# Attention scores as products of 64 rows, two heads at a time, with q and k turned before they are split

## The chip, the cores and the metric

One core of one Trainium2 chip. The metric is the device time of one execution in microseconds, the median of several runs. TensorE is PE, VectorE is DVE, ScalarE is ACT, GpSimd is POOL, and SyncE (SP) issues most of the transfers.

## The reference

Three layers follow one another: windowed attention, a mixture of eight experts with one expert per token, and a dense layer with a cosine. The change touches the attention alone.

```python
batch, n_heads, seq, head_dim = (4, 8, 576, 64)      # all float32

def _attn_ref(q, k, v):
    scores = scale * np.matmul(q, k.transpose(0, 1, 3, 2))
    rel = pos[:, None] - pos[None, :]
    bias = slopes[:, None, None] * (-np.abs(rel))[None, :, :]
    mask = (rel >= 0) & (rel < 128)
    scores = np.where(mask, scores + bias[None], -1000000000.0)
    attn = np.exp(scores - np.max(scores, axis=-1, keepdims=True))
    attn = attn / (np.sum(attn, axis=-1, keepdims=True) + 1e-09)
    return np.matmul(attn, v)

x = attn_out.transpose(0, 2, 1, 3).reshape(B * S, H * D)
x = _moe_ref(x, ...)      # logits, argmax, relu(x @ w1[e]) @ w2[e], weighted
return _moe2_ref(x, ...)  # h = x @ w_in;  (h * cos(h)) @ w_out
```

## The kernel before

**Units.** The attention is cut into 36 units (`units`): two pairs of batches (`bp`), nine row tiles of 128 tokens (`s`), two groups of four heads (`hg`). Tile `s == 4` joins the last 64 rows of both batches of a pair. Because of the window of 128, most units see two key tiles, the first and last tile of a batch one, the joined tile three (`nv` in `score`). Four units, one pair of tiles, end with the logits of 256 tokens. The expert stage can start only when the attention is done, since the tokens are sorted by expert first.

**Two-part numbers.** A float32 is held as the sum of two float32r numbers, high and low, so that a product on TensorE keeps nearly all its bits. `split` (L629) makes the two parts of q and k with two POOL instructions on rows of tokens, 128x512 each, into `qk`, where a head's 64 high and 64 low parts lie side by side. `tr` (L637) then turns each head on PE, one turn of 128 by 128 per head: 4 for q (L646), 4 for k (L653). The result has high parts in partitions 0 to 63 and low parts in 64 to 127. For q a second copy with high and low exchanged is needed: ACT copies the turned bank (L647), DVE copies one half exchanged (L649), ACT the other (L650); k takes one ACT copy (L654).

**Scores.** `score(n, hp)` (L656) does two of a unit's four heads. One head takes two products of 128 rows (L669): high with high and low with low in the first, the crossed ones in the second. For two key tiles the two heads share a bank: DVE merges the far key tile's columns into the near one's (L679), so that each token has 128 values. Then DVE adds the bias, takes the minimum and writes `sx` (L690, for each head), and ACT takes the exponential (L697).

**Turning and the product with v.** `flip(n, hp)` (L701) turns the exponentials of two heads on PE (L710, or L726 for one or three key tiles), ACT copies them to `pa` (L711, or L728), and POOL cuts them into the two triangles that belong to the two key tiles (L712, L714, 128x256 each). `pv(n, hp)` (L732) makes the products with v (L740); after the second half of a unit DVE divides by the sum (L750, one for each unit) and SP stores x. Then x is turned (L769, every second unit), split, and multiplied with the gate weights (L782).

**What sets the order.** The loop at L834 goes through 72 half units: `score` of step i, `flip` of step i - 3, `pv` of step i - 5 (LF, LP), with loads, splits and turns four units ahead (`ahead`). The instructions are issued in the order a scheduler gives them on each engine, so that on PE the half units' pieces come interleaved. Pieces of later work (x's turns, logits, ranks) wait in the list `after`, one or two for each half step. When the 32nd unit is done, `early` (L252) joins that list: it chooses the first expert and issues the fetch of its rows (`gather`, POOL) and weights. Tiles wait for their buffers: the banks S, T and P have two buffers, O and L one.

Of the kernel before, what the change touches and what calls it, by code (L numbers as in the profile page):

```python
# [15 lines left out]
ALU = mybir.AluOpType  # L16
# [13 lines left out]
def kernel(  # L30
# [53 lines left out]
    ps = ctx.enter_context(tc.tile_pool(name="ps", bufs=1, space=PSUM))  # L84

    def bank(tag, shape, dt=F32, name="bk"):
        return ps.tile(shape, dt, name=name, tag=tag, bufs=2 if tag in "TSP" else 1)
# [379 lines left out]

    with ExitStack() as c:
# [9 lines left out]
        identr = ca.tile([128, 128], F32R, name="identr")  # L478
        MARK = {"id": nc.vector.tensor_copy(identr, ident)}
# [134 lines left out]
        R, SPL, KT, QT, X, ST, PT, O = {}, {}, {}, {}, {}, {}, {}, {}  # L614
# [14 lines left out]
        def split(n):  # L629
            r = R.pop(n)  # L630
            sp_ = SPL[n] = sp.tile([128, 8, 2, D], F32R, name="qk")
            eng = nc.vector if n < 1 else nc.gpsimd
            eng.tensor_scalar(sp_[:, :, 0], r, 1.0, 0.0, op0=ALU.mult, op1=ALU.add)
            MARK["pool" if n else "dve"] = eng.tensor_tensor(sp_[:, :, 1], r, sp_[:, :, 0].bitcast(F32),
                                                             op=ALU.subtract)

        def tr(n):  # L637
            bp, s, hg = units[n]
            if s == 0:
                KT[bp, hg] = ktp.tile([128, 4, 9 * 128], F32R, name="kT")  # L640
            sp_ = SPL.pop(n)
            qT = sp.tile([128, 4, 2, 128], F32R, name="qT", bufs=6)
            QT[n] = qT
# [12 lines left out]
        def score(n, hp):  # L656
# [6 lines left out]
            nm = sm.tile([128, 2], F32, name="nm")  # L663
            sx = []

            def products(sc, j):
                h = 2 * hp + j
                for a in range(2):
                    nc.tensor.matmul(sc, QT[n][:, h, a], KT[bp, hg][:, h, 128 * t0:128 * t0 + w],  # L669
                                     start=a == 0, stop=a == 1)  # L670

            if nv == 2:


                both = bank("S", [128, 2, 256])
                for j in range(2):
                    products(both[:, j], j)
                own, other = (slice(128, 256), slice(0, 128)) if s < 4 else (slice(0, 128), slice(128, 256))
                nc.vector.copy_predicated(both[:, :, other], near.unsqueeze(1).to_broadcast([128, 2, 128]),  # L679
                                          both[:, :, own])  # L680
                w0, wv, bc = other.start, 128, 0
            for j in range(2):
                h = 2 * hp + j
                if nv == 2:
                    sc = both[:, j]
                else:
                    sc = bank("S", [128, 512])
                    products(sc[:, :w], j)
                x = sm.tile([128, 384], F32, name="sx")
                MARK["dve"] = nc.vector.tensor_tensor_reduce(  # L690
                    out=x[:, :wv], in0=sc[:, w0:w0 + wv], in1=bt[:, 4 * hg + h, bc:bc + wv], op0=ALU.add, op1=ALU.min,
                    scale=-0.125, scalar=3.0e38, accum_out=nm[:, j:j + 1])
                sx.append(x)
            p = []
            for j in range(2):
                e = sm.tile([128, 384], F32, name="e")
                MARK["act"] = nc.scalar.activation(e[:, :wv], sx[j][:, :wv], AF.Exp, bias=nm[:, j:j + 1], scale=-1.0)  # L697
                p.append(e)
            ST[n, hp] = (p, nv, t0 + f0)

        def flip(n, hp):  # L701
            p, nv, t0 = ST.pop((n, hp))
            heads = []
            if nv == 2:
                s = units[n][1]
                pp = bank("P", [128, 4, 128])
                pa = sm.tile([128, 2, 128], F32, name="pa", bufs=3)
                pT = sm.tile([128, 4, 128], F32, name="pT")
                for j in range(2):
                    nc.tensor.transpose(pp[:, j], p[j][:, 0:128], ident)  # L710
                nc.scalar.copy(pa, pp[:, 0:2])  # L711
                nc.gpsimd.affine_select(out=pT[:, 0:2], in_=pa, pattern=[[0, 2], [1, 128]], compare_op=ALU.is_ge,  # L712
                                        fill=0.0, base=0, channel_multiplier=-1)
                nc.gpsimd.affine_select(out=pT[:, 2:4], in_=pa, pattern=[[0, 2], [-1, 128]], compare_op=ALU.is_gt,  # L714
                                        fill=0.0, base=0, channel_multiplier=1)
                for j in range(2):
                    m = (pT[:, 2 + j], pT[:, j]) if s < 4 else (pT[:, j], pT[:, 2 + j])
                    heads.append((2 * hp + j, m))
                PT[n, hp] = (heads, nv, t0)
                return  # L720
            for grp in ([0, 1],) if nv < 3 else ([0], [1]):
                pp = bank("P", [128, 4, 128])
                pT = sm.tile([128, 4, 128], F32, name="pT")
                for gi, j in enumerate(grp):
                    for b in range(nv):
                        nc.tensor.transpose(pp[:, gi * nv + b], p[j][:, 128 * b:128 * b + 128], ident)  # L726
                m = len(grp) * nv
                nc.scalar.copy(pT[:, :m], pp[:, :m])  # L728
                heads += [(2 * hp + j, [pT[:, gi * nv + b] for b in range(nv)]) for gi, j in enumerate(grp)]
            PT[n, hp] = (heads, nv, t0)  # L730

        def pv(n, hp):  # L732
            bp, s, hg = units[n]
            heads, nv, t0 = PT.pop((n, hp))
            if hp == 0:
                O[n] = bank("O", [128, 4, 128])
# [5 lines left out]
            if hp == 0:  # L742
                return
# [651 lines left out]
```

## Time and profile before

| what | us |
|---|---|
| median of 3 runs (lowest, highest) | 860.01 (859.51, 861.32) |
| the profiled execution's own time | 857.24 |
| its span, first to last instruction | 855.5 |
| first unit's division starts | 25.3 |
| last unit's division starts | 196.0 |
| first turn of the expert stage starts | 200.5 |

The profiled execution took 1.7 us more than its span, and lies 2.8 us below the median of the three runs. A row of the lines view counts instructions of one kind: their busy time together, and the mean time of one. On PE the instructions overlap, because the ends are modelled and one matmul starts before the one before it has ended; what one costs PE is read from the distance between starts in the timeline, not from its mean time.

### The profile page before, as it was taken

What the parts mean: (1) busy time and instruction counts of PE and PEld (TensorE: products, weight loads), DVE (VectorE), ACT (ScalarE), POOL (GpSimd) and SP (SyncE); (2) the same over time, 40 slices, a digit from 0 to 9 for tenths busy, and PEclk for the clock granted to TensorE, in tenths of its full rate; (3) what the DMA queues carried; (4) which work ended last, traced back from release to release, by engine and by line L of the source; (5) the groups of instructions that cost most, each with busy time, mean ns of one, the idle gap of its engine ahead of it and who ended that gap; (6) DMA issues with size and microseconds to landing.
All of it is one profiled execution on the core that took longest, in us unless ns stands there. A gap on an engine that the chain in (4) does not pass through costs nothing. (4 is left out here: it accounts for less than half of the span.)

```text
span 855.5 us, 14987 instructions
## 1 busy us (share of the span) xinstructions
PE 809.7 (95%) x5269; PEld 721.3 (84%) x5269; DVE 633.4 (74%) x1496; ACT 528.1 (62%) x984; POOL 211.6 (25%) x275
## 2 busy tenths in 40 slices
PE   6899999997899999999899999999999999999996
PEld 6789988986889999999878778787788888888995
DVE  4867788776889999998657999897665555555562
ACT  6988888854356667675456576664544554445562
POOL 6765566420103223222000121111313001200100
PEclk9999999997999999999999999999999999999999
DMA  7354443108578878869733232410402001100000
GB/s 158 92 138 110 120 111 88 33 26 270 170 245 277 277 259 289 267 219 304 239 141 97 83 118 70 158 50 32 129 30 82 1 1 35 40 1 1 25 26 25
DMA packets 125136, 103.42 MB, mean 121 GB/s; under 512 B 61725, under 2 KB 105027, under 8 KB 125059
## 3 DMA queue, kind: packets, MB, share of 16 engines
q1 hardware_dynamic: 122099, 92.74, 35.7%
q0 software_dynamic: 2960, 9.70, 3.2%
q8 instruction: 42, 0.69, 0.3%
q14 instruction: 35, 0.29, 0.1%
HBM read 85.90 MB, written 16.52 MB: 120 GB/s over the span
## 5 line engine op out<-in xcount | busy, mean ns | idle before, releaser
L1009 PE MATMUL bk<-hh,s 128*128 128x256 f32 x864 | 117.8, 284 | 8.1 <-DVE y L1009 4.1
L1009 POOL TENSOR_TENSOR lf<-lf,mag 128x512 f32<-128x512 f32 x32 | 47.7, 1491 | 282.6 <-DVE mag L1009 261.0
L1009 PE MATMUL bk<-xT,s 128*128 128x256 f32 x864 | 115.0, 282 | 2.6 <-DVE s L1009 1.9
L1009 PEld LDWEIGHTS bk<-hh,s 128*128 128x128 f32 x864 | 108.0, 188 | 10.4 <-DVE y L1009 5.1
L1009 PEld LDWEIGHTS bk<-xT,s 128*128 128x128 f32 x864 | 107.3, 188 | 3.6 <-DVE s L1009 2.3
L1009 ACT CAST s<-r 128x1024 fp32r<-128x1024 f32 x72 | 75.1, 1050 | 56.1 <-DMA r<-in_moe_w_dram 37.0
L1009 PE MATMUL bk<-yT,wi_a 128*128 128x512 f32 (+1 forms) x480 | 104.3, 368 | 1.2 <-DVE yT L1009 0.8
L1009 DVE TENSOR_TENSOR s<-r,s 128x1024 fp32r<-128x1024 f32 x72 | 95.2, 1323 | 13.8 <-ACT s L1009 13.1
L1009 PE MATMUL bk<-yT,wi_b 128*128 128x512 f32 (+1 forms) x480 | 105.0, 368 | 0.0
L1009 ACT ACTIVATE r<-r 128x512 f32<-128x512 f32 (+1 forms) x80 | 47.2, 589 | 93.7 <-DVE r L1009 93.7
L1009 PEld LDWEIGHTS bk<-yT,wi_a 128*128 128x128 f32 x480 | 84.0, 188 | 17.1 <-DVE yT L1009 1.1
L1009 PEld LDWEIGHTS bk<-yT,wi_b 128*128 128x128 f32 x480 | 84.7, 188 | 15.6
L1009 DVE TENSOR_TENSOR r<-bk,r 128x512 f32<-128x512 f32 (+1 forms) x80 | 50.9, 636 | 61.5 <-ACT r L1009 61.0
L1009 PE MATMUL bk<-wo_b,gg 128*128 128x512 f32 x384 | 93.7, 392 | 1.6 <-DVE po L1009 1.0
L1009 PE MATMUL bk<-wo_a,gg 128*128 128x512 f32 x384 | 92.4, 389 | 0.3 <-DVE gg L1009 0.3
L1009 PEld LDWEIGHTS bk<-wo_b,gg 128*128 128x128 f32 x384 | 71.4, 188 | 18.9 <-issue 1.3
L1009 PEld LDWEIGHTS bk<-wo_a,gg 128*128 128x128 f32 x384 | 72.0, 188 | 15.7 <-DVE gg L1009 0.7
L740 PE MATMUL bk<-vt,pT 128*128 128x65 f32 x544 | 71.5, 274 | 1.9 <-POOL pT L714 0.8
L1009 DVE TENSOR_TENSOR gg<-r,gg 128x512 fp32r<-128x512 f32 x64 | 46.0, 719 | 34.3 <-ACT gg L1009 34.3
L740 PEld LDWEIGHTS bk<-vt,pT 128*128 128x128 f32 x544 | 67.6, 194 | 3.2 <-issue 1.5
L669 PE MATMUL bk<-kT,qT 128*128 128x256 f32 (+2 forms) x288 | 61.9, 326 | 3.3 <-DVE nm L690 2.1
L1009 ACT CAST gg<-r 128x512 fp32r<-128x512 f32 x64 | 39.7, 620 | 41.0 <-DVE r L1009 39.8
(286 smaller groups left out, 1413.9 us busy)
## 6 DMA issues: line engine op xcount, KB each, us to landing
r<-in_moe_w_dram SPq DMA_DIRECT2D x72, 512.0 KB
y_dram<-y SPq DMA_DIRECT2D x19, 256.0 KB
rqk<-in_q_dram SPq DMA_DIRECT2D x32, 128.0 KB
rqk<-in_k_dram SPq DMA_DIRECT2D x32, 128.0 KB
vt<-in_v_dram SPq DMA_DIRECT2D x32, 128.0 KB
x_dram<-xt SPq DMA_DIRECT2D x16, 256.0 KB
f64x<-in_moe_w_in_dram SPq DMA_DIRECT2D x8, 512.0 KB
raw<-in_moe_w_dram SPq DMA_DIRECT2D x8, 512.0 KB
```

The source lines that it names most:

```text
L669: nc.tensor.matmul(sc, QT[n][:, h, a], KT[bp, hg][:, h, 128 * t0:128 * t0 + w], start=a == 0, stop=a == 1)
L740: nc.tensor.matmul(ot[:, h, 0:65], pT[b], vt_of(bp, t0 + b, hg)[:, 65 * h:65 * h + 65], start=b == 0, stop=b == nv - 1)
L1009: r = op(*args, **kwargs)
```

## The change

`tr` now turns the raw q and k: one turn of 128 by 128 float32 numbers holds two heads of 64, so 4 turns do the q and k of a unit's four heads. The turned bank is split afterwards. For the first two units ACT and DVE do that from the bank. For the others ACT copies the high part of q (128x256) and the whole bank (`rT`, 128x512), and POOL makes the high and low of k and the low of q from `rT`, three instructions of 128x256. `split`, the exchanged copies and `identr` are gone.

The two heads of a pair lie in partitions 0 to 63 and 64 to 127. `score` does a whole unit: for each pair of heads three products (high-high, high-low, low-high) of 64 rows, the two heads one after the other in the two halves, each into a bank of its own. That is 12 products of 64 rows where 8 of 128 rows were. DVE's work on the scores is the same in number and size; the merge takes the two heads of one half together. `flip` and `pv` do a whole unit too: one copy of 128x512 and two POOL cuts of 128x512 for the units with two key tiles.

The loop goes through units: `score(n)`, turns of unit n + 4, `flip(n - 1)`, `pv(n - 2)`, and `issue_after` holds the order of PE: the products of `score` stand behind all PE work of the step before, and the rest of the step stands behind them (for n < 33). From n = 33 on, a step takes up to four pieces of the list `after`. The banks S have three buffers, P one, until the attention is done.

```diff
+    banks(S=3, T=2, P=1, O=1)
...
         def tr(n):
...
-            pt = bank("T", [128, 4, 128], F32R)
-            for h in range(4):
-                nc.tensor.transpose(pt[:, h], sp_[:, h].rearrange("p a d -> p (a d)"), identr)
-            nc.scalar.copy(qT[:, :, 0], pt)
-
-            nc.vector.tensor_copy(qT[0:64, :, 1], pt[64:128])
-            nc.scalar.copy(qT[64:128, :, 1], pt[0:64])
-            pt = bank("T", [128, 4, 128], F32R)
-            for h in range(4):
-                nc.tensor.transpose(pt[:, h], sp_[:, 4 + h].rearrange("p a d -> p (a d)"), identr)
-            nc.scalar.copy(KT[bp, hg][:, :, 128 * s:128 * s + 128], pt)
...
+            pt = bank("T", [128, 4, 128])
+            for c in range(4):
+                nc.tensor.transpose(pt[:, c], r[:, 2 * c:2 * c + 2].rearrange("p a d -> p (a d)"), ident)
...
+            rT = sp.tile([128, 4, 128], F32, name="rT")
+            nc.scalar.copy(qT[:, 0], pt[:, 0:2])
+            nc.scalar.copy(rT, pt)
+            nc.gpsimd.tensor_scalar(kT[:, 0], rT[:, 2:4], 1.0, 0.0, op0=ALU.mult, op1=ALU.add)
+            nc.gpsimd.tensor_tensor(kT[:, 1], rT[:, 2:4], kT[:, 0].bitcast(F32), op=ALU.subtract)
+            MARK["pool"] = nc.gpsimd.tensor_tensor(qT[:, 1], rT[:, 0:2], qT[:, 0].bitcast(F32), op=ALU.subtract)
...
-                for a in range(2):
-                    nc.tensor.matmul(sc, QT[n][:, h, a], KT[bp, hg][:, h, 128 * t0:128 * t0 + w],
-                                     start=a == 0, stop=a == 1)
...
+                for p in pairs:
+                    for a, b in ((0, 0), (0, 1), (1, 0)):
+                        for j in range(2):
+                            rs = slice(64 * j, 64 * j + 64)
+                            with ExitStack() as w_:
+                                for ins in TURN if n < 33 else ():
+                                    w_.enter_context(tc.issue_after(ins.ins))
+                                TURN.clear()
+                                nc.tensor.matmul(sc[j][:, p - pairs[0], :w], qT[rs, a, p], kT[rs, b, p],
+                                                 start=a == 0 and b == 0, stop=a == 1)
...
+            for pairs in ([0, 1],) if nv < 3 else ([0], [1]):
+                sc = [bank("S", [128, 2, 256] if nv < 3 else [128, 1, 512]) for j in range(2)]
+                products(sc, pairs)
...
+                nc.scalar.copy(pT, pp)
...
+                nc.gpsimd.affine_select(out=tri_[0], in_=pa, pattern=[[0, 4], [1, 128]], compare_op=ALU.is_ge,
                                         fill=0.0, base=0, channel_multiplier=-1)
...
-        LF, LP = 3, 5
...
+        LF, LP = 1, 2
...
+        for n in range(N + LP):
+            if n < 3:
+                ahead(n, dt=n + 1)
+            if n < N:
+                score(n)
+            with ExitStack() as w:
+                if n < 33:
+                    w.enter_context(tc.issue_after(TURN[-1].ins))
+                setups(2 * n)
+                if n > 1:
+                    ahead(n + 1)
+                pops(1 if n < 33 else 2)
+                if LF <= n < N + LF:
+                    flip(n - LF)
+                setups(2 * n + 1)
+                if n >= LP:
+                    pv(n - LP)
+                pops(2 if 33 <= n < N + LP - 1 else 1)
+
+    nc = tc.nc
+    banks(S=2, T=2, P=2, O=1)
```

**The order on PE**, in the middle of the attention where tiles with one key tile are done. `kT,qT` are scores, `identr,qk` or `ident,rqk` the turns of q and k, `ident,e` the turns of the exponentials, `vt,pT` the products with v, `ident,xt` the turns of x. Before:

```order
L669 MATMUL bk<-kT,qT 128x256 x4
L710 MATMUL bk<-ident,e 128x128 x2
L653 MATMUL bk<-identr,qk 128x128 x4
L646 MATMUL bk<-identr,qk 128x128 x4
L653 MATMUL bk<-identr,qk 128x128 x4
L669 MATMUL bk<-kT,qT 128x256 x4
L710 MATMUL bk<-ident,e 128x128 x2
L740 MATMUL bk<-vt_139,pT 128x65 x4
L769 MATMUL bk<-ident,xt 128x128
```

Now (the line is that of the recording helper for all of them):

```order
L487 MATMUL bk<-kT,qT 128x256 x12
L487 MATMUL bk<-ident,rqk 128x128 x4
L487 MATMUL bk<-ident,e_1867 128x128 x4
L487 MATMUL bk<-vt_139,pT 128x65 x4
L487 MATMUL bk<-kT,qT 128x256 x12
L487 MATMUL bk<-ident,rqk 128x128 x4
L487 MATMUL bk<-ident,e_1956 128x128 x4
L487 MATMUL bk<-vt_140,pT 128x65 x4
L487 MATMUL bk<-ident,xt 128x128 x4
L487 MATMUL bk<-kT,qT 128x256 x12
```

The scores of a unit stand in one block, and each block stands between turns that use all 128 rows; all other work of the step follows in one fixed order.

**The order on ACT**, two steps of units with two key tiles. `e` are exponentials, `pa` copies of their turned form, `qT`, `kT`, `rT` copies of turned q and k, `xT` of turned x. Before:

```order
L697 ACTIVATE e<-sx,nm 128x128 x2
L650 COPY qT<-bk 64x4x128
L711 COPY pa<-bk 128x256
L697 ACTIVATE e<-sx,nm 128x128 x2
L647 COPY qT<-bk 128x4x128
L711 COPY pa<-bk 128x256 x2
L697 ACTIVATE e<-sx,nm 128x128 x2
L770 CAST xT_95<-bk 128x4x128
L650 COPY qT<-bk 64x4x128
L697 ACTIVATE e<-sx,nm 128x128
L654 COPY kT<-bk 128x4x128
```

Now:

```order
L679 CAST qT<-bk 128x256
L680 COPY rT<-bk 128x512
L727 ACTIVATE e_1365<-sx,nm 128x128 x4
L741 COPY pa<-bk 128x512
L789 CAST xT_98<-bk 128x4x128
L679 CAST qT<-bk 128x256
L680 COPY rT<-bk 128x512
L727 ACTIVATE e_1444<-sx,nm 128x128 x4
```

The one copy `pa` of a unit stands behind the four exponentials of the unit after it: the copy behind `e_1365` is that of the unit before `e_1365`, whose turns PE has behind the scores of `e_1365`.

## Rows read from the trace of the kernel before

**Rows 1.** Page, part 1: busy time of each engine over the span.
```profile
PE 809.7 (95%) x5269; PEld 721.3 (84%) x5269; DVE 633.4 (74%) x1496; ACT 528.1 (62%) x984; POOL 211.6 (25%) x275
```

**Rows 2.** Windows: width, busy us (instructions) PE, PEld, DVE, ACT, POOL, PEclk, DMA.
```profile
40.00:160.00 120.00, 115.06 (x1024) 107.31 (x1023) 91.65 (x428) 101.05 (x246) 71.16 (x115) 1.00 0.42 105
...
195.00:205.00 10.00, 5.78 (x27) 3.88 (x26) 5.06 (x8) 4.69 (x7) 0.85 (x1) 0.59 1.03 354
```

**Rows 3.** Timeline, DVE: the first and last unit's division (36 in all).
```profile
25.30 0.41 DVE L750 TENSOR_TENSOR xt<-bk,den 128x256 f32<-128x256 f32 x1
...
195.99 0.42 DVE L750 TENSOR_TENSOR y<-bk,den 128x256 f32<-128x256 f32 x1
```

**Rows 4.** Lines, each shape apart, 40 to 160 us: busy us, mean ns of one.
```profile
L697 ACT ACTIVATE e<-sx,nm 128x128 f32<-128x128 f32 x79 | 29.6, 404 | 4.5 <-DVE nm L690 0.9 <-PE bk L726 0.9 <-ACT qT L647 0.7
...
L647 ACT CAST qT<-bk 128x512 fp32r<-128x512 f32 x25 | 14.6, 585 | 1.3 <-PE bk L646 1.3
...
L650 ACT CAST qT<-bk 64x512 fp32r<-64x512 f32 x24 | 13.9, 578 | 1.4 <-DVE qT L649 0.8
...
L711 ACT COPY pa<-bk 128x256 f32<-128x256 f32 x33 | 11.9, 367 | 3.2 <-PE bk L710 3.1
...
L690 DVE CUSTOM_DVE_ANT_0 sx<-bk,bias 128x128 f32<-128x128 f32 x77 | 20.3, 283 | 3.8 <-ACT kT L654 1.1 <-PE bk L726 1.1 <-PE bk L669 1.0
L649 DVE CAST qT<-bk 64x512 fp32r<-64x512 f32 x25 | 17.3, 693 | 4.1 <-ACT qT L647 3.4
...
L679 DVE COPY_PREDICATED bk<-near,bk 128x256 f32<-128x256 uint8 x30 | 12.6, 421 | 2.8 <-PE bk L669 2.4
...
L750 DVE TENSOR_TENSOR xt<-bk,den 128x256 f32<-128x256 f32 x24 | 10.0, 417 | 0.2
...
L633 POOL TENSOR_SCALAR qk<-rqk 128x512 fp32r<-128x512 f32 x24 | 14.9, 622 | 26.1 <-PE bk L653 26.0
...
L634 POOL TENSOR_TENSOR qk<-rqk,qk 128x512 fp32r<-128x512 f32 x25 | 31.9, 1277 | 1.9
...
L712 POOL TENSOR_SCALAR_AFFINE_SELECT pT<-pa 128x256 f32<-128x256 f32 x33 | 13.6, 414 | 22.4 <-ACT pa L711 19.8 <-DMA rqk<-in_q_dram 1.5 <-DMA rqk<-in_k_dram 1.0
...
L669 PE MATMUL bk<-kT,qT 128*128 128x256 f32 x151 | 30.0, 306 | 1.2 <-DVE nm L690 1.0
```

**Rows 5.** Timeline, PE: runs of one kind and the next start.
```profile
100.54 0.50 PE L653 MATMUL bk<-identr,qk 128*128 128x128 f32 x4
100.88 0.59 PE L669 MATMUL bk<-kT,qT 128*128 128x256 f32 x3
101.40 1.08 PE L740 MATMUL bk<-vt,pT 128*128 128x65 f32 x8
102.29 0.36 PE L669 MATMUL bk<-kT,qT 128*128 128x256 f32 x1
...
103.29 0.72 PE L669 MATMUL bk<-kT,qT 128*128 128x256 f32 x4
103.85 0.38 PE L726 MATMUL bk<-ident,e 128*128 128x128 f32 x2
104.07 0.38 PE L769 MATMUL bk<-ident,xt 128*128 128x128 f32 x2
```

**Rows 6.** Timeline, PE: products of 16 rows between products of 128.
```profile
109.78 0.26 PE L653 MATMUL bk<-identr,qk 128*128 128x128 f32 x1
109.97 0.29 PE L789 MATMUL bk<-ident,ls 16*128 16x16 f32 x2
110.19 0.28 PE L653 MATMUL bk<-identr,qk 128*128 128x128 f32 x1
110.30 0.60 PE L669 MATMUL bk<-kT,qT 128*128 128x256 f32 x3
```

**Rows 7.** Timeline, PE: the first instructions of the expert stage.
```profile
200.47 1.11 PE L1009 MATMUL bk<-ident,xg 128*128 128x128 f32 x4 [3.32 <-DMA xg<-x_dram,idx]
201.24 2.06 PE L1009 MATMUL bk<-xT,wg 128*16 128x256 f32 x8
```

More of the change, by code (lines that the diff above doesn't have):

```diff
@@ L682, in score @@
[L682 to L712, printed above, removed]
+            kT, qT = KT[bp, hg][:, :, :, 128 * t0:128 * t0 + w], QT.pop(n)
@@ new lines, in score @@
+            todo = []
+            for pairs in ([0, 1],) if nv < 3 else ([0], [1]):
+                sc = [bank("S", [128, 2, 256] if nv < 3 else [128, 1, 512]) for j in range(2)]
+                products(sc, pairs)
+                for j in range(2):
+                    if nv == 2:
+                        own, other = (slice(128, 256), slice(0, 128)) if s < 4 else (slice(0, 128), slice(128, 256))
+                        nc.vector.copy_predicated(sc[j][:, :, other], near.unsqueeze(1).to_broadcast([128, 2, 128]),
+                                                  sc[j][:, :, own])
+                        w0, wv, bc = other.start, 128, 0
+                    for p in pairs:
+                        h = 2 * p + j
+                        x = sm.tile([128, 384], F32, name="sx")
+                        MARK["dve"] = nc.vector.tensor_tensor_reduce(
+                            out=x[:, :wv], in0=sc[j][:, p - pairs[0], w0:w0 + wv], in1=bt[:, 4 * hg + h, bc:bc + wv],
+                            op0=ALU.add, op1=ALU.min, scale=-0.125, scalar=3.0e38, accum_out=nm[:, h:h + 1])
+                        MARK["act"] = nc.scalar.activation(e[:, h, :wv], x[:, :wv], AF.Exp, bias=nm[:, h:h + 1],
+                                                           scale=-1.0)
@@ L719, in flip @@
-                PT[n, hp] = (heads, nv, t0)
+                if units[n][1] < 4:
+                    tri_ = tri_[::-1]
+                PT[n] = ([[t[:, h] for t in tri_] for h in range(4)], t0)
                 return
[L721 to L729, printed above, removed]
@@ L730, in flip, with pv @@
-            PT[n, hp] = (heads, nv, t0)
-        def pv(n, hp):
-            bp, s, hg = units[n]
-            heads, nv, t0 = PT.pop((n, hp))
-            if hp == 0:
-                O[n] = bank("O", [128, 4, 128])
-            ot = O[n]
-            for h, pT in heads:
-                for b in range(nv):
+            PT[n] = ([[pTs[(nv * h + b) // 4][:, (nv * h + b) % 4] for b in range(nv)] for h in range(4)], t0)
+        def pv(n):
+            bp, s, hg = units[n]
+            heads, t0 = PT.pop(n)
+            ot = bank("O", [128, 4, 128])
+            for h, pT in enumerate(heads):
+                for b in range(len(pT)):
@@ L807, in logits, with ahead @@
             return [products, choose, lambda: ranks(t)]
-        done = {"l": 0, "s": 0, "t": 0}
-        def ahead(n, dl=5, ds=4, dt=4):
-            for key, fn, d in (("l", load, dl), ("s", split, ds), ("t", tr, dt)):
+        done = {"l": 0, "t": 0}
+        def ahead(n, dl=5, dt=4):
+            for key, fn, d in (("l", load, dl), ("t", tr, dt)):
                 while done[key] < min(N, n + d):
@@ L815, in ahead @@
                     done[key] += 1
-            if done["s"] == N and not RP:
+            if done["t"] == N and not RP:
                 rawc.close()
                 RP.append(pool(bc, "rp", 2, "right"))
-        LF, LP = 3, 5
-        steps = [(n, hp) for n in range(N) for hp in range(2)]
+        LF, LP = 1, 2
         after = []
@@ L825 @@
             nc.vector.memset(vt.rearrange("p (h e) -> p h e", e=65)[:, :, D:65], 1.0)
-        ahead(0, 3, 0, 0)
+        ahead(0, 3, 0)
         todo = setup_bias(bias)
@@ L831, with setups @@
             tables = setup_tables()
-        with behind("id", "dve", "pool"):
-            ahead(0, 5, 3, 1)
-        for i in range(len(steps) + LP):
-            if i < len(steps):
-                n, hp = steps[i]
-                if hp == 0:
-                    ahead(n, dt=1 if n == 0 else 2 if n == 1 else 4)
-                score(n, hp)
+        with behind("dve", "pool"):
+            ahead(0, 5, 1)
+        def setups(i):
             if i == 1:
@@ L853, with pops @@
                     todo.pop(0)()
-            if LF <= i < len(steps) + LF:
-                flip(*steps[i - LF])
-            if after:
-                after.pop(0)()
-            if i >= LP:
-                pv(*steps[i - LP])
-            if i >= 69 and after:
-                after.pop(0)()
+        def pops(count):
+            for _ in range(count):
+                if after:
+                    after.pop(0)()
+        LATER = []
+        for n in range(N + LP):
[18 more added lines that the diff above has]
+    banks(S=2, T=2, P=2, O=1)
     wres = pool(ctx, "wres", 1)
```

92 lines of the change are left out of this document (56 added, 36 removed).

## The prediction

> **What bounds the kernel now.** I first read the page for the busy shares [rows 1]: PE is busy for 95% of the span. That share is not a limit by itself, because matmuls overlap and a waiting one can count as busy. So I went to the windows of the attention, the only stage that the change touches [rows 2], with the timeline of DVE for the pace [rows 3]. The first unit's division starts at 25.30 and the thirty-sixth at 195.99, so a unit takes 170.69 / 35 = 4.88 us. Between 40 and 160 us, 24 units end (the x24 of L750 [rows 4]); in that window a unit costs ACT 101.05 / 24 = 4.21 us, DVE 91.65 / 24 = 3.82 and POOL 71.16 / 24 = 2.97. The granted clock is 1.00 there and the DMA share 0.42, so neither presses.
>
> For PE I count what a unit must cost, from distances between starts [rows 5]. Four turns of q or k parts take 100.88 - 100.54 = 0.34, so 0.085 each. Four score products take 103.29 to 103.85, so 0.14 each. A float32 turn takes (104.07 - 103.85) / 2 = 0.11, and a product with v (102.29 - 101.40) / 8 = 0.111. A unit with two key tiles then needs 8 x 0.085 + 8 x 0.14 + 4 x 0.11 + 8 x 0.111 = 0.68 + 1.12 + 0.44 + 0.89. Add 0.22 for its half of x's four turns and 0.40 for its share of logits and ranks (an estimate: two products a unit at 0.14 and some small ones). The sum is 3.75 us of 4.88. So PE is not the engine that sets the pace, in spite of its 95%. ACT has the most work, 4.21 us, and the pace is 4.88 / 4.21 = 1.16 times that: the surplus is waiting between engines that are all close to full. The reader should see in [rows 4] that ACT's copies of q and k (L647, L650, and one of L647's shape for k) are the largest share of ACT's work after the exponentials.
>
> **The change, part by part.** The unit with two key tiles is the usual one; I price it and apply it to all 35 distances.
>
> ACT loses two copies of 128x512 at 0.585, one of 64x512 at 0.578 and two of 128x256 at 0.367 [rows 4], 2.48 us. It gains a copy of 128x256 (0.367, as L711) and two of 128x512 (the bank to `rT`, and the one `pa`), 0.585 each as L647: 1.54 us. ACT's work falls by 0.94 to 3.27 us.
>
> DVE loses the exchanged copy L649, 0.693 us, and falls to 3.13 us. The merge and the bias step stay as they were in size and number.
>
> POOL loses L633 and L634, 1.90 us, and gains three instructions of half their size: 0.31 + 2 x 0.64 = 1.59. Its four cuts of 128x256 (0.414 each) become two of 128x512. No row shows one of that size; the bounds are 0.41 (all fixed cost) and 0.83 (all by size). I take 0.83, since L633 and L634 of 512 columns show that POOL's work grows with size. POOL falls to about 2.66 us.
>
> PE loses 8 turns at 0.085 and gains 4 at 0.11: -0.24. The scores are the open price: 8 products at 0.14 (1.12 us) become 12 products of 64 rows and 256 columns, which no row shows. The lower bound is that two heads run side by side in the two halves: 6 x 0.14 = 0.84 us. The upper bound is that they follow one another as if of 128 rows: 12 x 0.14 = 1.68. Between them stands 12 x 0.085 = 1.02, the distance of the turns in [rows 5], as the least that a weight load with a short product takes. I take 1.02: the halves can overlap in streaming, but each product still loads weights.
>
> Beside it, the array changes between 128 and 64 rows twice in a unit. The nearest rows are the products of 16 rows [rows 6]: the turn before them starts 0.19 us ahead where 0.085 is usual, a surplus of 0.1, and the two themselves take 0.22, no more than two float32 turns. I take 0.1 for each change, 0.2 a unit; the bounds are 0 and 0.306, the whole mean time of a score product [rows 4]. PE's work is then 3.75 - 0.24 - 1.12 + 1.02 + 0.2 = 3.61 us (3.43 with the lower bound of the scores, 4.27 with the upper).
>
> The Trainium skill speaks against this change here: "TensorEngine Tiling", Key Properties, says that a change of the tiling mode drains the engine, and the change makes two in every unit. By the surplus of 0.1 in [rows 6] the trace shows only a part of such a drain; by the rule the price is the upper bound, and the result is the second rival below. The skill's "TensorE: Matmul & The Clock Gate", Part 3, says that products in different row groups run at the same time; no row here shows that, and by it the scores would cost the lower bound.
>
> New waits: PE's order is now fixed for each step. What stands behind a waiting product is all of PE. The longest chain is: scores of n end; DVE merges and adds bias for four heads, 2 x (0.421 + 2 x 0.283) = 1.97; the last exponential 0.40; then `pa` of unit n - 1, which ACT has behind it, 0.585; two cuts, 1.66; then the products of n - 1 with v. That is 4.6 us from the end of one unit's scores to a product in the next step. The ring closes over two units: 4.6 + 0.89 for the products with v, 0.22 for x, 1.02 and 0.2 for the scores after next, 6.9, or 3.5 us a unit plus the hand-overs. It is below PE's 3.61, so it is covered, but not by much. SP's loads and stores keep number, size and their turn in SP's queue (the load of unit n + 5 and the store of unit n - 2 in step n, where it was n + 4 and n - 3); a load's buffer now comes free by PE's turns instead of POOL's split. At the new pace the DMA share would be 0.42 x 5.0 / 4.19 = 0.50 (120 us / 24 units is 5.0 in that window), so I cost them at nothing. If loads came late, the turns of q and k would show it, with all of PE behind them.
>
> **The sum.** The largest work for each unit was 4.21 us (ACT) and becomes 3.61 (PE). With the same factor 1.16 a unit takes 4.19 us, 0.69 less; times 35 this is 24 us. The start I leave as it is: the first two units still need two copies and subtractions before their scores. The end too: 3.32 us of waiting for the gathered rows [rows 7] may be covered in part, since `early` issues the fetch in the step of unit 34 instead of 35, so 0 to 3.3 us more. The expert and dense stages are moved earlier as they are, with the same banks. The profiled execution's 857.24 would become 833; the median of the runs shown lies 2.8 above it at 860.01, so I forecast **836 us**.
>
> **The rivals.**
>
> 1. *The halves do not run side by side.* Scores cost 1.68, PE 4.27 us a unit, more than ACT had. With a surplus between nothing and 1.16 the pace is 4.27 to 4.95: 21 us faster to 2 us slower, about 850. For it: nothing in this trace shows two products at once. Against: the two heads write different banks and use different partitions. Chance 0.18.
>
> 2. *Every change of the array's rows empties it, and the fixed order lets nothing cover it (slower).* Two changes at 0.306 and scores at 1.68 give PE 2.39 (all but the scores) + 1.68 + 0.61 = 4.68, with 1.16 a pace of 5.43: 35 x 0.55 = 19 us slower, 879. It decides from the point where PE's work passes 4.88 / 1.16 = 4.2 us a unit. Against: only 0.1 of it in [rows 6]. Chance 0.07. This is the drain of "TensorEngine Tiling" of the Trainium skill.
>
> 3. *The clock falls.* The window of 195 to 205 us has 0.59 [rows 2], so a part of it at 1.2 GHz, after PE had waited for the gathered rows; eight products of 256 columns there take 2.06 us [rows 7], 0.26 each against 0.14. If the attention ran so, PE would need 3.61 x 0.26 / 0.14 = 6.7 us a unit, 64 us slower in all, 924. Against: PE has more than half of each unit to do, and 1.00 is granted in all of 40 to 160. Chance 0.02.
>
> 4. *The time is given back behind the attention*, because the first expert's weights or gathered rows land no earlier: 855 to 860. Against: both are issued from the attention's own last steps. Chance 0.05.
>
> 5. *The surplus shrinks too*, since ACT and DVE have 0.94 and 0.69 us less and PE 0.84 for the scores: 3.43 x 1.10 = 3.77, 39 us faster, with the end's 3.3 us 818. Chance 0.08.
>
> **How the numbers follow.** The forecast has 0.60 (a pace of 3.9 to 4.5, so 826 to 847). The range is 818 to 854: rival 5 below, and above it rival 1 with a surplus of 1.10 (4.70, 6 us faster); outside remain rivals 2 to 4 and the edges of 1 and 5. About 0.2%, 1.7 us, is what a measurement of this kernel can tell from no change. Faster: 0.60 + 0.08 + 0.14 of rival 1 + 0.02 of rival 4 = 0.84. The same: 0.02 + 0.03 = 0.05. Slower: 0.02 + 0.07 + 0.02 = 0.11.
>
> **What would show it.** Right: divisions 4.0 to 4.4 us apart; 12 score products from start to start in 0.9 to 1.3 us; ACT near 3.3 us a unit; the expert stage starts at about 176 instead of 200.5 and lasts as long as before. Wrong: a score block of over 1.5 us (rivals 1 and 2), a distance of 0.3 before or behind the block (2), a granted clock below 1.00 before 160 us (3), or products with v that wait for POOL's cuts in every step, which would mean that the ring of 6.9 us is longer than I count.

## The result and the profile after

The changed kernel takes **866.14 us** (859.09 to 873.78, 14 runs), the kernel before 860.27 in the same comparison (858.46 to 863.48, 14 runs). The ratio is 1.0053, 95% interval 1.0028 to 1.0078: slower by half a per cent where 836 us was forecast. The profiled execution after took 869.51 us with a span of 867.5. Executions of the changed kernel lie further apart than those of the kernel before, and follow the granted clock (mean 0.984 in the execution of 859 us, 0.966 in one of 874); ratios leave out executions that lie over 1.5% above the fastest of their kernel (one of these 14), medians are of all.

Part 1 of the page after answers to [rows 1]; it looks the same and tells nothing of the loss:
```profile
PE 813.3 (94%) x5269; PEld 714.0 (82%) x5269; DVE 612.9 (71%) x1461; ACT 493.3 (57%) x912; POOL 200.4 (23%) x259
```
The windows of the changed kernel (width, then busy us and instructions of PE, PEld, DVE, ACT, POOL, then PEclk, DMA share, GB/s) answer to [rows 2]:
```profile
20.00:200.00 180.00, 159.76 (x1408) 141.35 (x1408) 111.81 (x602) 104.83 (x267) 83.93 (x145) 0.93 0.34 86
...
40.00:160.00 120.00, 107.17 (x949) 94.19 (x947) 74.45 (x383) 70.72 (x180) 59.05 (x99) 0.94 0.43 106
60.00:98.00 38.00, 34.38 (x330) 30.91 (x327) 23.04 (x123) 22.66 (x58) 18.56 (x31) 1.00 0.44 108
```
ACT, DVE and POOL did lose work: 101.05, 91.65 and 71.16 us became 70.72, 74.45 and 59.05. Part of that is only that 22 units end in the window (divisions of L769) instead of 24: a unit costs ACT 3.21 us, DVE 3.38 and POOL 2.68, where it cost 4.21, 3.82 and 2.97. But PE does 949 instructions in the 120 us, where it did 1024; it idles for 12.8 us instead of 4.9, and its clock is 0.94 instead of 1.00. The pace is in DVE's timeline (start, duration), against [rows 3]:
```profile
19.95 0.42 DVE L769 TENSOR_TENSOR xt<-bk,den 128x256 f32<-128x256 f32 x1
...
206.18 0.42 DVE L769 TENSOR_TENSOR y<-bk,den 128x256 f32<-128x256 f32 x1
```
That is (206.18 - 19.95) / 35 = 5.32 us a unit, where 4.88 was and 4.19 was forecast. The attention starts 5.35 us earlier and ends 10.2 later; the expert stage's first turn starts at 209.53 instead of 200.47.

PE's timeline at full clock shows what a unit is now (start, duration; in brackets the wait ahead of it and who ended it):
```profile
79.77 0.97 PE L487 MATMUL bk<-kT,qT 64*128 64x256 f32 x12
80.67 0.66 PE L487 MATMUL bk<-ident,rqk 128*128 128x128 f32 x4
81.17 0.60 PE L487 MATMUL bk<-ident,e 128*128 128x128 f32 x4
81.61 1.90 PE L487 MATMUL bk<-vt,pT 128*128 128x65 f32 x16
83.43 0.98 PE L487 MATMUL bk<-kT,qT 64*128 64x256 f32 x12
84.34 0.66 PE L487 MATMUL bk<-ident,rqk 128*128 128x128 f32 x4
84.84 0.60 PE L487 MATMUL bk<-ident,e 128*128 128x128 f32 x4
85.27 1.90 PE L487 MATMUL bk<-vt,pT 128*128 128x65 f32 x16
87.01 0.39 PE L487 MATMUL bk<-ident,xt 128*128 128x128 f32 x2
88.09 0.44 PE L487 MATMUL bk<-ident,xt 128*128 128x128 f32 x2 [0.70 <-DVE xt L769]
88.46 0.97 PE L487 MATMUL bk<-kT,qT 64*128 64x256 f32 x12
89.37 0.66 PE L487 MATMUL bk<-ident,rqk 128*128 128x128 f32 x4
89.78 1.17 PE L487 MATMUL bk<-xT,wg 128*16 128x256 f32 x8
90.78 0.60 PE L487 MATMUL bk<-ident,e 128*128 128x128 f32 x4
```
Three things stand in it. The scores of four heads take 0.90 us from their first start to the turn behind them, less than forecast. The products with v are 16 records and take 1.82 us a unit, not 0.89. And the turn of x, right behind the products that make x, waits for DVE's division with all of PE behind it. Over the stretch from 60 to 200 us PE's waits (total, times, longest) put that first:
```profile
PE bk L487 <- DVE xt L769: 10.0, 12, 1.2
PE bk L487 <- DVE nm L724: 2.0, 3, 1.0
```

PE's own need for a unit after can be summed from such rows: scores 0.90, q and k 0.50, turns of the exponentials 0.44, products with v 1.82, x 0.38 (two turns of each half, without the idle time), logits 1.00 / 4 = 0.25, and 0.11 for the small turns and ranks: **4.40 us**. In e5 below x's four turns follow one another without a wait and take 0.44, 0.22 a unit, so up to 0.16 of this is still the wait. The profiled loss then comes apart, against the 833 that the forecast had for the profiled execution; its 4.19 us a unit were a need of 3.61 and a surplus of 0.58 for waits:
- PE's need is 4.40, not 3.61: 35 x 0.79 = 27.7 us.
- The clock: 0.93 over the 180 us, so 12.6 us at most.
- Waits: (186.23 - 12.6) / 35 = 4.96 a unit at full clock, 0.56 over the need, no more than the surplus of 0.58 that the forecast allowed: -0.7 us.
- The earlier start: -5.35. Behind the attention: the first turn comes 3.35 instead of 4.48 us after the last division, -1.1, and from there to the end it takes 658.0 instead of 655.0, +3.0.

The sum is 36.2 us; 869.5 - 833 is 36.5. The waits are what is left over, so the sum closes by itself. What bears the split out is PE's idle time in the windows: 20.2 of 180 us after, near to 35 x 0.56 = 19.6, and 9.2 of 168 in the kernel before:
```profile
25.00:193.00 168.00, 158.82 (x1418) 147.82 (x1417) 129.06 (x632) 135.00 (x335) 90.31 (x154) 1.00 0.35 90
```

### The profile page after: what moved, and what is told of

Read it like the earlier page. It is cut to its first block, busy times and chain, and to the rows that moved or that the text cites. A ratio compares the mean times of both kernels' runs of the same rounds, so it can differ in the third digit from the quotient of the medians.

```text
span 867.5 us, 14736 instructions
## 1 busy us (share of the span) xinstructions
PE 813.3 (94%) x5269; PEld 714.0 (82%) x5269; DVE 612.9 (71%) x1461; ACT 493.3 (57%) x912; POOL 200.4 (23%) x259
## 5 line engine op out<-in xcount | busy, mean ns | idle before, releaser
L1042 DVE SCALAR_TENSOR_TENSOR r<-ki,bk 128x512 f32<-128x512 int32 (+1 forms) x80 | 50.4, 631 | 15.9 <-ACT ki L1042 15.3
```

Of the source, the lines that this page charges most:

```text
L1042: r = op(*args, **kwargs)
```

## The experiments

Two explanations were to be told apart: PE waits in an order that is now fixed; or the products of 64 rows cost something themselves, in time or in clock. Behind them stood a question on the forecast: was PE, against its argument, the engine that set the pace before?

**e1_late_x.** The turn of x one step later, so that it no longer stands behind the products that it needs:
```diff
+                waiting = len(after)
                 if n >= LP:
                     pv(n - LP)
-                pops(2 if 33 <= n < N + LP - 1 else 1)
+                pops(min(1, waiting) if n < 33 else 2 if n < N + LP - 1 else 1)
```


> The changed kernel, but the turn of x of a unit is issued one step after its products with v, between the turns of q and k and those of the exponentials, instead of right behind them. Theory A (PE waits in the fixed order, and the clock falls because PE waits): the turns of x, which cost 22 us of PE in the changed kernel outside the low clock against 10 at their usual distance, fall to about 7 to 10; fewer stretches at 1.2 GHz before 200 us than the five seen; 12 to 25 us faster than the changed kernel, 842 to 854. Theory B (the clock falls because of the 64-row products and the changes between 64 and 128 rows): the five stretches stay and the time moves by less than 5 us.

Measured: 870.34 us (868.04 to 872.69), ratio 1.0124 (1.0095 to 1.0154), slower still. A window of this run, and PE's waits from 60 to 200 us:
```profile
20.00:200.00 180.00, 158.84 (x1394) 140.92 (x1394) 108.86 (x593) 102.45 (x265) 84.21 (x145) 0.93 0.34 86
...
PE bk L487 <- DVE ohb L824: 8.7, 5, 2.0
PE bk L487 <- DVE xT L790: 4.5, 5, 1.1
PE bk L487 <- DVE nm L724: 1.0, 2, 0.5
```
The wait for `xt` is gone, and two others of the same queue (`after`: x's turn, the logits, the choice of experts, the ranks) have taken its place. No single step was late; with one place for the queue behind the products with v, whatever stands there waits for the step ahead of it. By the expectation this is the outcome of theory B (five stretches at 1.2 GHz stay, the clock is 0.93 as in the changed kernel, the time moves by 4 us); but the waits stayed as well, 14.9 us where they were 12.6, so e1 does not tell the two theories apart. e4 does.

**e2_free_order.** The edges that hold PE in program order left out (both `issue_after` of `TURN` never entered).

> The changed kernel without the edges that hold PE's order; the scheduler then puts part of the turn of x among the scores and leaves the rest almost as it is. Theory A: a part of the wait in front of the turn of x goes, 3 to 10 us faster than the changed kernel. Theory A2 (the block of scores itself, held together, makes the waits): over 15 us faster. Theory B: no change within 3 us.

Measured: 869.17 us (859.7 to 876.46, four executions 17 us apart), so no gain or loss can be told. Two windows of the profiled one:
```profile
29.00:66.00 37.00, 37.00 (x158) 30.09 (x157) 14.44 (x88) 16.28 (x39) 12.15 (x21) 0.50 0.33 78
70.00:190.00 120.00, 117.34 (x1092) 104.02 (x1091) 80.38 (x428) 77.81 (x201) 61.37 (x103) 1.00 0.36 93
```
At full clock the waits are all but gone (PE idles for 2.7 of 120 us), but one stretch of 37 us ran at 1.2 GHz with PE busy throughout and ate the gain. So the fixed order makes waits, and the clock is a second matter: here it fell without a fixed order.

**e3_one_half.** The loop over the two halves outside the loop over the parts, so that three products of one half follow one another:
```diff
-                    for a, b in ((0, 0), (0, 1), (1, 0)):
-                        for j in range(2):
+                    for j in range(2):
+                        for a, b in ((0, 0), (0, 1), (1, 0)):
```


> The changed kernel with the three products of one head issued after one another, then those of the other head, so that neighbours lie in the same half of the array. If neighbours in different halves run side by side, the 12 products take 1.1 to 1.5 us instead of 0.91 and the kernel is 5 to 18 us slower than the changed kernel. If a 64-row product simply costs less, the block stays at 0.9 and the time too.

Measured: 867.1 us (858.93 to 872.22), ratio 1.0058 (1.002 to 1.0097), as the change itself. The scores' block at full clock (PE's timeline):
```profile
102.45 0.98 PE L487 MATMUL bk<-kT,qT 64*128 64x256 f32 x12
103.36 0.66 PE L487 MATMUL bk<-ident,rqk 128*128 128x128 f32 x4
```
0.91 us as before. By the expectation this means that a product of 64 rows simply costs less, wherever its neighbour lies; that reading was wrong. The single starts in this trace lie in pairs, the first two at 102.448 and 102.458 us, though the program has three products of one half ahead of the other's. PE starts a product of the other half ahead of its turn, and e10 below shows the same.

**e4_before_fixed.** The kernel before, its attention's PE instructions chained in program order; all products keep 128 rows:
```diff
+                with ExitStack() as c:
+                    if Chain.on and Chain.last is not None:
+                        c.enter_context(tc.issue_after(Chain.last.ins))
+                    r = getattr(tc.nc.tensor, name)(*args, **kwargs)
+                Chain.last = r
```


> The kernel before with PE held to the order in which the program is written (half units, all products of 128 rows). Theory A: PE waits as in the changed kernel, the granted clock falls in some stretches before 190 us although there is no 64-row product, and the kernel is 10 to 30 us slower than before, 870 to 890. Theory B: waits, but the clock stays at 1.00 until 190 us; under 10 us slower.

Measured: 900.41 us (898.74 to 904.85), ratio 1.0477 (1.0448 to 1.0506), slower than even theory A expected. Windows:
```profile
40.00:200.00 160.00, 142.51 (x1060) 132.93 (x1058) 97.47 (x447) 107.26 (x253) 70.59 (x114) 0.83 0.31 78
113.00:133.00 20.00, 19.65 (x104) 19.04 (x104) 8.27 (x45) 9.57 (x24) 6.22 (x11) 0.51 0.23 57
```
Without one product of 64 rows PE idles for 17.5 of 160 us and the granted clock is 0.83. The low clock of the changed kernel needs no 64-row products to come about; waits in a fixed order are enough. The second window shows that PE can also be busy through a stretch at 1.2 GHz with products of 128 rows alone.

**e7_no_exchange.** The kernel before without the two copies to the other half, L649 on DVE and L650 on ACT, which the forecast counted as 0.693 and 0.578 us a unit; the scores use `QT[n][:, h, 0]` twice:
```diff
-            nc.vector.tensor_copy(qT[0:64, :, 1], pt[64:128])
-            nc.scalar.copy(qT[64:128, :, 1], pt[0:64])
```


> The kernel before with less work on ACT and DVE alone: the two exchanged copies of q (L649, L650) are left out, so ACT has 0.58 and DVE 0.69 us less for each unit, and the second product of a head takes the same q as the first; PE has the same instructions. Tokens may go to other experts, so the attention is compared: its last division at 196.0 and the expert stage at 200.5 us before. The prediction's reading (ACT sets the pace, PE needs 3.75 us a unit): 15 to 25 us earlier. Theory A (PE was full, 4.6 of 4.88 us, since a product with v is two records): within 4 us of before.

**e8_one_tile.** The kernel before with `for b in range(1)` in the products with v: PE loses 128 of the 272 products, about 28 us at 2 x 0.111 each.

> The kernel before with less work on PE alone: only the first key tile's product with v is made, so 256 of 544 records at 0.11 us are left out, 28 us in all; ACT, DVE and POOL do the same. The attention is compared, as tokens may go to other experts. The prediction's reading (ACT sets the pace): the last division within 4 us of 196.0. Theory A (PE was full): 15 to 25 us earlier, until ACT's 4.2 us a unit holds it.

Measured: 852.6 us (850.55 to 855.76), ratio 0.9935 (0.9912 to 0.9957) for e7, and 851.1 (849.08 to 853.57), ratio 0.9923 (0.9895 to 0.9951) for e8. The same window and the last division, of e7, then of e8:
```profile
40.00:160.00 120.00, 116.88 (x1066) 111.67 (x1067) 80.11 (x406) 88.74 (x223) 74.10 (x120) 1.00 0.45 110
...
189.83 0.42 DVE L747 TENSOR_TENSOR y<-bk,den 128x256 f32<-128x256 f32 x1
```
```profile
40.00:160.00 120.00, 108.10 (x919) 96.05 (x918) 99.46 (x459) 108.20 (x266) 75.21 (x124) 0.99 0.43 108
...
183.80 0.42 DVE L750 TENSOR_TENSOR y<-bk,den 128x256 f32<-128x256 f32 x1
```
The expectations go by the attention alone, since tokens may go to other experts behind it. Its last division, at 195.99 before, comes 6.2 us earlier in e7 and 12.2 in e8. Both lie between the two expectations, nearer to the one that PE was full (within 4, and 15 to 25). With ACT and DVE relieved, by the forecast's argument the pace should have followed ACT; PE is busy for 97% instead. With PE relieved ACT and PE are at 90% each. Neither relief brought what was taken away (35 x 0.578 = 20 us of ACT's and 35 x 0.693 = 24 of DVE's time in e7, 28 of PE's in e8): both PE and ACT were nearly full before, and a large gain needs both to lose work.

**e5_spread.** The change with the queue's steps spread: none behind the products with v, two in every fourth step ahead of the turns of the exponentials. Order still fixed.
```diff
-                pops(1 if n < 33 else 2)
+                pops((2 if n % 4 == 1 else 1) if n < 33 else 2)
...
-                pops(2 if 33 <= n < N + LP - 1 else 1)
+                pops(0 if n < 33 else 2 if n < N + LP - 1 else 1)
```


> The changed kernel with each later piece (turn of x, logits, their turn, ranks) in a step of its own, one step behind the piece it needs, all in front of the turns of the exponentials; PE's order held as in the changed kernel. Theory A (the waits in the fixed order come from pieces that stand right behind what they need, and the clock falls because PE waits): PE's own work is about 4.2 us a unit with 16 product records with v, the waits shrink to under 0.3, a unit takes 4.3 to 4.6 us, at most one stretch at 1.2 GHz between 30 and 190 us, 20 to 35 us faster than the changed kernel, 832 to 847. Theory B (64-row products or the changes of rows lower the clock): the waits shrink, but low stretches of 20 us and more in sum stay between 20 and 200 us; 850 to 862.

Measured: **849.28 us** (847.48 to 851.53), ratio 0.9885 (0.9855 to 0.9915): faster than both kernels, and between the two expectations (832 to 847, and 850 to 862), nearer to theory A's. PE's waits from 60 to 180 us, then the first and last division:
```profile
PE bk L487 <- DVE nm L724: 2.6, 2, 1.6
PE bk L487 <- DVE ohb L824: 1.0, 2, 0.5
PE bk L487 <- DVE xT L790: 0.3, 1, 0.3
...
19.32 0.42 DVE L769 TENSOR_TENSOR xt<-bk,den 128x256 f32<-128x256 f32 x1
...
185.61 0.42 DVE L769 TENSOR_TENSOR y<-bk,den 128x256 f32<-128x256 f32 x1
```
3.9 us in 120, where the change had 12.6 and e1 14.9 in 140; the clock is 0.97 from 20 to 185 us. One edit of where a queue is served, with the products, copies and cuts of the change untouched, is worth 15 us by the ratios, 17 by the medians. A unit takes (185.61 - 19.32) / 35 = 4.75 us, not the 4.3 to 4.6 expected, and only 0.13 less than before. So more than half of the 11 us won on the kernel before is the start: the first division comes 25.30 - 19.32 = 6.0 us earlier. No run shows which part of the change brought that.

**e6_spread_free.** e5 without the fixed order.

> The same without the edges that hold PE's order. Theory A: within 5 us of the version with held order, since hardly anything is left to wait for. Theory A2 (holding the score block together makes waits of its own): 5 to 15 us faster than the version with held order.

Measured: 858.16 us (845.14 to 866.61, ten executions), 2 us under the kernel before and 9 above e5, where either no difference or a gain on e5 was expected: a miss. Windows of the execution of 866.61:
```profile
27.00:74.00 47.00, 46.76 (x203) 39.58 (x204) 19.74 (x104) 17.49 (x43) 16.09 (x28) 0.50 0.32 75
94.00:188.00 94.00, 92.67 (x890) 83.89 (x892) 69.75 (x369) 62.57 (x163) 53.45 (x88) 1.00 0.34 88
```
From 94 to 188 us 21 units take 4.47 us each with PE idle for 1.3 us in all: PE's own need, close to the 4.40 summed above, is the pace. But this execution spent 47 us at 1.2 GHz before that; the mean clock of the ten lies between 0.960 and 0.985, and the time follows it.

**e9_fill_128 and e10_fill_64.** e6 with two products of no use ahead of each unit's scores, 512 columns of bfloat16; their result is overwritten. In e9 they have 128 rows, in e10 64 (`bias[0:64, ...]`, both in the first half):
```diff
+                for _ in range(2 if pairs[0] == 0 else 0):
+                    nc.tensor.matmul(sc[0].rearrange("p a b -> p (a b)"), bias[0:128, 0, 0:128],
+                                     bias[0:128, 0:2].rearrange("p h c -> p (h c)"), start=True, stop=True)
                 products(sc, pairs)
```


> The version with spread pieces and free order (median 858, mean clock 0.960 to 0.985 by execution, 47.8 us in one stretch at 1.2 GHz in its profile), with two extra products of 128 rows and 512 columns in front of each unit's scores, whose results are overwritten: 0.43 us of PE a unit, 15 us in all at 2.4 GHz. Theory B2 (the clock, once down, stays down because the mix with 64-row products keeps too little of the array busy): the long low stretch goes, the mean clock is 0.98 and more in nearly every execution, 850 to 862. Theory A3 (only waits matter): low stretches of the same length, 865 to 880.

> The same with the two extra products of 64 rows, in one half of the array, with the same columns. Theory B2 (rows count): low stretches as without them, mean clock 0.96 to 0.975 in most executions, 865 to 880. Theory B3 (any dense streaming counts, rows do not): as with 128 rows.

Measured: 857.84 (855.0 to 861.13), ratio 0.9983 (0.9958 to 1.0009), and 859.55 (851.26 to 862.68), ratio 0.9982 (0.995 to 1.0014). The mean clock was 0.98 to 0.99 in both, so added products of 64 rows keep it up nearly as well as those of 128 (means of ten executions 0.984 and 0.987). Neither profiled execution has a stretch at 1.2 GHz as long as e6's: e9's clock is 0.50 from 30 to 33 us, e10's from 30 to 42. PE's timeline around them, of e9, then of e10:
```profile
120.65 0.59 PE L487 MATMUL bk<-bias 128*128 128x512 bf16 x2
121.18 0.97 PE L487 MATMUL bk<-kT,qT 64*128 64x256 f32 x12
```
```profile
123.99 0.39 PE L487 MATMUL bk<-bias 64*128 64x512 bf16 x1
123.99 0.38 PE L487 MATMUL bk<-kT,qT 64*128 64x256 f32 x1
124.21 0.38 PE L487 MATMUL bk<-bias 64*128 64x512 bf16 x1
124.22 1.07 PE L487 MATMUL bk<-kT,qT 64*128 64x256 f32 x11
```
In the program both added products stand ahead of the unit's twelve scores. In e10 the second starts 0.22 us after the first, its own half being busy, and in between PE has started a score product, within 0.01 us of the first. The two halves run side by side, and the other half's product is taken ahead of its turn. The Trainium skill, "TensorE: Matmul & The Clock Gate", Part 3, says that products in different row groups run at once, which agrees, and that they start in the program's order, which these rows don't bear out; the measurement decides. That is why e3's order made no difference.

**e11_fill_early and e12_fill_early_held.** e6 and e5 with e9's two products in the steps 1 to 10 alone (`if pairs[0] == 0 and 1 <= n <= 10`).

> The spread schedule in free order, with two products of 128 rows and 512 columns, whose result nothing reads, ahead of the scores of units 1 to 10 alone (20 products, 0.216 us apart in the run with fillers in every unit: 4.3 us of PE's time). C1 (the long stretch at 1.2 GHz that some executions of the spread schedule have early in the attention begins because PE's work is thin and full of waits there, and dense streaming in the early units keeps it away): the executions lie close together, mean clock 0.975 to 0.99, 844 to 852, all within 1%. C2 (it begins by chance, or the fillers must go on to keep the clock): executions between 846 and 870 as in the spread schedule without fillers, with a stretch of more than 20 us at 0.50 in some.

> The same 20 products of no use in the spread schedule with the change's fixed order. C1: 846 to 851, since the spread schedule in fixed order already keeps the clock (849.28, 847 to 852) and the fillers cost up to 4.3 us and save some short stretches at 0.50. C2: 851 to 856, the fillers' time on top.

Measured: e11 **848.84 us** (847.53 to 850.9), ratio 0.9864 (0.9836 to 0.9892); e12 851.79 (847.99 to 860.26), ratio 0.9907 (0.9878 to 0.9935), at the edge between its two expectations. Windows of e11:
```profile
34.00:41.00 7.00, 6.78 (x35) 5.34 (x35) 3.74 (x29) 3.12 (x9) 1.90 (x3) 0.51 0.20 57
41.00:184.00 143.00, 139.37 (x1296) 123.98 (x1296) 100.28 (x526) 92.12 (x238) 72.81 (x120) 1.00 0.38 95
184.00:202.00 18.00, 13.73 (x81) 11.23 (x82) 11.42 (x41) 6.94 (x9) 2.13 (x2) 0.53 0.87 291
```
With 20 products of no use the free order keeps full clock from 41 to 184 us, and its four executions lie within 0.4%. e11 and e5 are the fastest two; their intervals overlap, and both beat both kernels. In the held order the added products bring nothing.

## Why the prediction was wrong, and where it was right

**The step that failed first: PE's need.** "8 x 0.111" for the products with v took each record of [rows 5] for a product: a unit with two key tiles has 4 x 2 = 8 products, and each float32 product is two records. The page of the kernel before had it, in part 5:
```profile
L740 PE MATMUL bk<-vt,pT 128*128 128x65 f32 x544 | 71.5, 274 | 1.9 <-POOL pT L714 0.8
```
The program's 36 units have 272 such products; 544 records are two of each. The term is 16 x 0.111 = 1.78, PE's need before 4.64 of 4.88 us, and the 95% of [rows 1] that the prediction talked away was right; the timeline puts a wait down as idle time, not as busy. e7 bears it out: less work for ACT and DVE alone brought the attention's end forward by 6.2 us, not by the 15 to 25 of the prediction's reading. In the 0.79 us a unit by which the need was off, this term alone is 0.93 too small (1.82 against 0.89); the scores, priced 0.32 too dear, give some of it back. With this term put right, the prediction's own prices give 4.50 after, and with the surplus of 4.88 / 4.64 a pace of 4.73: 5 us faster, 855.

**The step that failed second: the waits.** "It is below PE's 3.61, so it is covered": the ring was not what closed; from 60 to 200 us PE never waits for POOL's cuts. The queue `after` was, which the prediction priced as work (0.22 for x, 0.40 for logits and ranks) and not as waits: x's turn stands behind the products that make x, with all of PE behind it. The prediction asked of the fixed order only what one ring costs, not who stands behind each wait. e1 moved the waits, e5 took most of them away. They cost some 20 us of the profiled execution. That the forecast's surplus was as large is luck: its factor of 1.16 came from needs that were too small. Against the kernel before (4.88 - 4.64 = 0.24 a unit) the waits grew by 0.32 a unit, 11 us.

**The step that failed third: the clock.** Rival 3 was put at 0.02 since 1.00 was granted in all of 40 to 160 us before. PE had hardly waited there; with a fixed order it waits, and the clock falls to 0.94, or 0.83 in e4. By e4 the fixed order alone is enough for that, and e5, with the same products and fewer waits, has 0.97, so it was probably, in the main, a consequence of the second step. The Trainium skill, "TensorE: Matmul & The Clock Gate", Part 1, describes kernels whose clock falls because PE waits between groups of products, and e4's 0.83 agrees. Over the 14 executions of the changed kernel 0.01 of the mean clock goes with 6.7 us. What in the early units of e6 brought its 47 us at 1.2 GHz, with PE busy for 46.76 of them, stays open: a wait of 1.71 us for POOL's cut ended at 27.24 us, as the stretch began, but no run leaves out that wait alone. Nor does a run exclude that products of 64 rows help to keep the clock down once it has fallen; the kernel before, in free order too, shows no such stretch. Rival 3's own reading was off as well: in the kernel before the clock falls ahead of the wait for the gathered rows, which began at 200.47 - 3.32 = 197.15 us:
```profile
193.00:197.10 4.10, 3.00 (x12) 2.29 (x12) 1.61 (x6) 1.04 (x1) 2.13 (x2) 0.51 0.99 299
```

**Right: the scores and the changes of rows.** 12 products with the changes around them were put at 1.02 + 0.2; the block is 0.90 with the change behind it, and the pairs start together. Rival 1 falls by e10. For the change of rows, e9's two products of 128 rows and the change behind them take 121.18 - 120.65 = 0.53 us; at 0.22 a product 0.1 is left, the size taken. The single starts in the traces make it a little more, since the start behind comes late as well. From the last product with v to the second distinct start of the scores it is 0.43 us after (at 83.43) and 0.285 before (at 103.29); from the last score product to the second turn behind it is 0.37 after (at 84.34) and 0.23 before (at 103.85). That is 0.14 a change. The drain of the Trainium skill's "TensorEngine Tiling", Key Properties, is there, then, but a small one. Rival 2, the slower one, named the fixed order but gave it the wrong cause and 879.

**Right in direction: the other engines.** ACT and POOL came to 3.21 and 2.68 us a unit, where 3.27 and 2.66 were forecast; DVE to 3.38, where 3.13 was, so it lost 0.44 of the 0.69 priced. Lines of the changed kernel, 40 to 160 us (busy us, mean ns of one), which answer to [rows 4]:
```profile
L683 POOL TENSOR_TENSOR qT<-rT,qT 128x256 fp32r<-128x256 f32 x23 | 16.8, 729 | 1.7 <-ACT rT L680 1.7
...
L680 ACT COPY rT<-bk 128x512 f32<-128x512 f32 x23 | 13.5, 588 | 0.0
...
L745 POOL TENSOR_SCALAR_AFFINE_SELECT pT<-pa 128x512 f32<-128x512 f32 x15 | 9.6, 638 | 0.8 <-ACT pa L741 0.5
```
The copies of 128x512 are 0.585 as taken, POOL's cuts 0.64, between the bounds of 0.41 and 0.83, its subtractions 0.73 where 0.64 was taken. DMA was in no wait of PE in the attention but one of 0.3 us. The gathered rows were covered when the attention ended late; in e5, which ends early, PE waits 2.97 us for them, so the 0 to 3.3 us left open at the end are not won. The start, which the forecast left as it is, brought 5.35 us: without that the result would have been as much slower.

## What to carry to other kernels

Count an engine's work by records of one run against the program's own count before a 95% busy share is explained away; a factor of two in one term turned "not the bound" into "the bound". When an engine's order becomes fixed, go through the order and ask of each instruction whether what it needs is made by the step right ahead of it: a side queue served in the wrong place of the loop cost 15 to 17 us here, more than the change brought at its best (11 us). Waits in TensorE's queue can cost clock as well, so read the granted clock of a stretch ahead of its busy times.

## What the runs showed of the hardware that was not expected

- PE runs products in its two row halves side by side and takes a product of the idle half ahead of the program's order (e10: starts at 123.99, 123.99, 124.21, 124.22 us; e3: pairs 0.01 us apart).
- PE can be busy without a break at 1.2 GHz for long: 46.76 of 47.00 us in e6, 37.00 of 37.00 in e2, and 19.65 of 20.00 at 0.51 in e4, which has no product of 64 rows. With e9's two added products in each unit no execution had a mean clock under 0.98.
- A float32 product stands as two records, 0.11 us apart for 65 columns (544 records of 272 products); a float32 turn as one, and so does a float32r product of the scores.
